# New planning figures and shorter turns in a planned convolution and gated feed-forward kernel

## The chip, the cores and the metric

The kernel runs on one core of a Trainium2 chip. The metric is the device time of one execution in microseconds (us). Before the change it is 1277.85 us, the median of three runs (1277.19, 1277.85 and 1282.22). Engines are named as in the profile: PE is TensorE (PEld its weight loads), DVE is VectorE, ACT is ScalarE, POOL is GpSimd, SP is SyncE, which here issues every DMA.

## The reference

Two stages follow each other. The first is a causal convolution whose seven weights are different at each position and head: a softmax over seven numbers, and with it a weighted sum of the last seven rows of `x`. The second is a gated feed-forward layer over the result.

```python
# x: (4, 4096, 192), weight_gen: (4, 4096, 8 heads, 7)
w = exp(weight_gen - max over the 7); w = w / (sum of w + 1e-9)
out[b, s, h] = sum over k of w[b, s, h, k] * x_pad[b, s + k, h]       # 24 channels a head
# x becomes (16384, 192); w_gate and w_val are (192, 1536), w_out is (1536, 192)
result = (sigmoid(x @ w_gate) * (x @ w_val)) @ w_out
```

## The kernel before

**Tiling.** The 16384 positions are cut into 32 blocks of 512. The 1536 hidden columns are cut into 12 groups of 128. A *unit* is one block with one group. The first groups of blocks 0 and 1 are done in halves of 256 positions, three groups of block 0 and four of block 1, so there are 391 units in all. Every fp32 operand of a matmul is split into a rounded value and its remainder, and a product takes three matmuls: a unit has 28 matmuls of 64 rows, which run as 14 pairs, one in the lower and one in the upper half of the array's rows.

**Stages of a block.** The convolution makes the block's inputs. DVE multiplies shifted slices of `x` by the weights (`prod`, L772; for the first positions L798) and adds the products (L710). For three early tiles the adding is done on PE, by matmuls with an identity matrix (`f_sum`, L720). The sums are then cast and split: channels 0 to 127 go to `A`, with the halves swapped to `As`, and the other 64 channels go to `T`. ACT casts (L828, L848, L875, L895), DVE subtracts to get the remainder (L831, L878), and ACT copies the remainder to the other rows (L851, L898). From block 4 on DMAs do the swaps.

**A period of PE.** PE takes one unit after another. In period s it makes gate and value of unit s (18 matmuls on `A`, `As`, `T`) and, beside them, the output products of unit s-3 (10 matmuls on `hh`, `hl`). Gate and value of a unit have a PSUM bank each (tiles `gv`), and there are two such pairs. So unit s can start only when ACT has read the gate of unit s-2 (sigmoid, L1041) and DVE has read its value (the product with the sigmoid, L1044). The product is cast to `hh` (ACT, L1047), and the remainder `hl` is a subtraction (DVE, L1050).

**Weights.** They arrive as 64-bit floats. Each of the 12 groups has a raw tile (`raw`, L410) that is turned into fp32 by 11 instructions: two on ACT (L419, L422), six on DVE (L426 to L457), one cast on ACT (L463) and two subtractions on DVE (L467), which leave the tile `W`.

**The softmax** of a stretch of positions is made on DVE and ACT (L516 to L555, exponential in L533) and stored to DRAM (`ws`, L584). The weights of a block come back spread over the heads' channels as `wb` and `wt` (L668).

**Turns.** Since the weights come one group at a time, the first two blocks take turns: block 0 does groups 0 to 6, then block 1 does groups 0 to 6, then block 0 the groups 7 to 11 and block 1 the same. From block 2 on a block does its 12 groups in one go. `TURN = 7` says so.

**What sets the order.** A planner (`Plan`) is run when the program is built. Every operation has a guessed duration on its engine, what it depends on, the buffers that it takes and a due time; the planner plays the program through with these guesses, and takes for each engine the operation that can start first, among those within 0.1 us of it the one due first. What comes out is a fixed order of instructions on each engine: an engine that meets an instruction whose input is missing waits, and all behind it wait with it. For DMAs the planner counts a start-up time, a bandwidth and an end time, and issues a load no more than `AHEAD` before the queue is expected to be free of the one before. The figures steer the order alone; no instruction takes another time because of them.

**Fills.** While a gap is planned on PE in the first 130 us, it is filled for 0.65 of its planned length by matmuls on a constant tile (`blank`): L628 before the first output products, L980 after.

Of the kernel before, what the change touches and what calls it, by code (L numbers as in the profile page):

```python
# [39 lines left out]
class Plan:  # L40
# [8 lines left out]
    SAME = {"pe": 0.0, "act": 0.05, "dve": 0.13, "pool": 0.1, "sp": 0.0}  # L49
    WINDOW = 0.1  # L50
    BANDWIDTH = 190e3
    DMA_START, DMA_END = 0.6, 1.0
    MARGIN, EARLY, LATE = 2.5, 60.0, 6.0
    AHEAD = 1.5
    TABLE = 1.28
    APART = 3

# [177 lines left out]
def conv_gated_ffn(ctx: ExitStack, tc: tile.TileContext, xt, wg, wcat, outT):  # L235
# [13 lines left out]
    P = 128  # L249
# [56 lines left out]
    def act(n, psum=False):  # L306
        return (0.05 if psum else 0.093) + 0.000835 * n
# [16 lines left out]
    def slot(n):  # L324
        return (n + 32) / 2400

    SP = 0.55
    RAW, WB = 0.6, 3.5

    def op(engs, fn, deps=(), **kw):  # L330

# [9 lines left out]
    EARLY_BLOCKS = 4  # L341
    FILL, WARM = 130.0, 4.8
    units = []
    TURN = 7
    spans = [(n, f, g) for f, g in ((0, TURN), (TURN, NF)) for n in range(2)]
    for n, first, end in spans + [(n, 0, NF) for n in range(2, NB)]:
        apart, cuts_ = parts(n)
# [272 lines left out]

    blank = sb.tile([P, 2 * N], F32R, name="blank")
    zero, ones = blank[:, :P], blank[:, N:]
    spare = plan.places["pt"][1]["buf"][:, M2:]
    begun = []

    def idle(buf, t):
        for _ in range(0 if begun else int(t / slot(K * CH))):
            nc.tensor.matmul(  # L628
                spare[:, : K * CH], ones[:, :P], ones[:, : K * CH], start=True, stop=True
            )  # L630

    def spread(key, chunks, sel, deps):
# [48 lines left out]
    def taps(key, groups, cols, mult, deps, uses, first=True, port=True, at=0, bank_of=None):  # L681
# [32 lines left out]
        if bank_of:  # L714
            for i, (k, z) in enumerate(groups):
                multiply(i)

                def f_sum(buf, e, i=i, k=k, z=z):
                    for j in range(k, z):
                        nc.tensor.matmul(  # L720
                            out(buf), eye[:, 0].bitcast(F32), flat(buf, i, j - k, j - k + 1),
                            start=j == 0, stop=j == K - 1,
                        )

                last = op(
                    {"pe": 0.1 + 0.00085 * (z - k) * cols}, f_sum, [ms[-1]] + ([last] if i else []),
                    alloc=[] if i else [(bank_of, ACC)], uses=[keys_[i]] + ([ACC] if i else []),
                )
                last.fill = idle
            return ACC, last  # L730
# [76 lines left out]
    def attention(n, a, z):  # L807
# [22 lines left out]
        def f_lo(buf, e):  # L830
# [3 lines left out]
            )  # L834

        hi = op(
            {"act": act(C)}, f_hi, last, alloc=[("A", A), ("As", As)] if new else [],
            uses=[ACC] + ([] if new else [A]),
        )
        lo = op(both(C), f_lo, [hi], uses=[A, ACC])  # L840
# [1 line left out]
        for rows, to in ((LOW, UP), (UP, LOW)):  # L842
            if n >= EARLY_BLOCKS:
                done.append(swap(A, As, all_, all_, rows, to, [lo]))
                continue

            def f_shi(buf, e, rows=rows, to=to):
                nc.scalar.copy(buf[As][to, 0, all_], buf[ACC][rows, :C])  # L848

            def f_slo(buf, e, rows=rows, to=to):  # L850
                nc.scalar.copy(buf[As][to, 1, all_], buf[A][rows, 1, all_].bitcast(F32))  # L851

            done.append(op({"act": act(C)}, f_shi, last, uses=[As, ACC], after=[hi]))
            done.append(op({"act": act(C)}, f_slo, [lo], uses=[A, As]))

        ready[q, 0], ready[q, 1] = [hi, lo], done

# [13 lines left out]
        for i, rows in enumerate((LOW, UP)):  # L871
            own = slice(a + i * M2, a + (i + 1) * M2)

            def f_thi(buf, e, rows=rows, own=own):
                nc.scalar.copy(buf[T][rows, 0, own], buf[ACT_][rows, :M2])  # L875

            def f_tlo(buf, e, rows=rows, own=own):
                ENG[e].tensor_tensor(  # L878
                    out=buf[T][rows, 1, own], in0=buf[ACT_][rows, :M2],
                    in1=buf[T][rows, 0, own].bitcast(F32), op=ALU.subtract,  # L880
                )

            fresh = new and not i
            his.append(
                op({"act": act(M2)}, f_thi, lastt, alloc=[("T", T)] if fresh else [],
                   uses=[ACT_] + ([] if fresh else [T]), after=his[-1:])
            )
            los.append(op(both(M2), f_tlo, [his[-1]], uses=[T, ACT_]))
            to = UP if i == 0 else LOW
            if n >= EARLY_BLOCKS:  # L890
                done.append(swap(T, T, own, own, rows, to, [los[-1]]))
                continue

            def f_shi(buf, e, rows=rows, to=to, own=own):
                nc.scalar.copy(buf[T][to, 0, own], buf[ACT_][rows, :M2])  # L895

            def f_slo(buf, e, rows=rows, to=to, own=own):
                nc.scalar.copy(buf[T][to, 1, own], buf[T][rows, 1, own].bitcast(F32))  # L898

            done.append(op({"act": act(M2)}, f_shi, lastt, uses=[T, ACT_], after=[his[-1]]))  # L900
            done.append(op({"act": act(M2)}, f_slo, [los[-1]], uses=[T]))
        ready[q, 2] = done + his + los


# [186 lines left out]
    def evac(n, done):  # L1091
# [19 lines left out]
            nc.sync.dma_start(out=outT[P:D, b * S + t0 : b * S + t0 + N], in_=buf[OT][LOW, :N])  # L1111

        t = due_block(n)
        h = op({"act": act(N, True)}, f_head, done, alloc=[("osb", OH)], uses=[PH], due=t + 8, lag=8)
        c = op({"act": act(N, True)}, f_shift, done, alloc=[("ev", EV)], uses=[PT], due=t + 10, lag=10)
        a = op({"dve": dve(N)}, f_fold, [c], port=False, alloc=[("osb", OT)], uses=[PT, EV], due=t + 14, lag=4)
        op({"sp": SP}, f_sth, [h], uses=[OH], nbytes=P * N * 4, due=t + 18, lag=10)
        op({"sp": SP}, f_stt, [a], uses=[OT], nbytes=R * N * 4, due=t + 20, lag=10)
# [89 lines left out]
```

## Time and profile before

| | |
|---|---|
| median of three runs | 1277.85 us |
| the profiled execution | 1276.69 us |
| its span, first to last instruction | 1274.9 us |
| PE busy | 1262.1 us, 99% of the span |
| DVE busy | 1010.1 us, 79% |
| ACT busy | 610.2 us, 48% |
| granted clock of PE | 0.999 of full speed |

The span is the stretch that the trace covers; the execution's own time is 1.8 us longer. DVE's 79% is a mean over two very different parts: it is busy for nine tenths or more of nearly every slice up to 300 us, and for seven to eight tenths behind that. POOL's 1499 instructions are almost all one-element writes that mark the change between the two halves of PE's rows (L958).

### The profile page before, as it was taken

The page shows a single profiled execution, that of the slowest core. Times are in us where ns is not written, and L with a number is a line of the kernel's source. Part 1 is how long each engine was busy: PE and PEld are TensorE (multiplying, and loading weights), DVE is VectorE, ACT ScalarE, POOL GpSimd, SP SyncE. Part 2 cuts the span into 40 slices and gives each one's busy share as a digit, 9 for nine tenths or more (in the row PEclk, how much of TensorE's full clock was granted, in tenths as well). Part 3 has the DMA queues.
Part 4 walks back from the last instruction along what each step waited for, and adds up shares of the span by engine and source line. Part 5 has one row for each costly group of instructions (what it writes and reads, how often), then busy time and mean ns, then how long its engine had stood idle before and what let it go on. Part 6 is the DMA issues. An engine that isn't in the chain of part 4 may idle for free.

```text
span 1274.9 us, 29675 instructions
## 1 busy us (share of the span) xinstructions
PE 1262.1 (99%) x11169; PEld 1124.4 (88%) x11169; DVE 1010.1 (79%) x1547; ACT 610.2 (48%) x1063; POOL 135.1 (11%) x1499
## 2 busy tenths in 40 slices
PE   8999999999999999999999999999999999999998
PEld 8887878888889999999999999999999999999997
DVE  8999999989998987788777788777778877755443
ACT  5766654454454644444444444444444444444443
POOL 0111111111111111111111111111111111111110
PEclk9999999999999999999999999999999999999999
DMA  8654687589878754454454454454454351011100
GB/s 237 198 117 110 149 168 144 154 171 180 169 143 207 156 148 111 113 137 105 104 123 107 113 137 111 99 123 108 111 137 117 92 129 35 20 32 38 38 14 13
DMA packets 44384, 150.37 MB, mean 118 GB/s; under 512 B 6288, under 2 KB 18896, under 8 KB 40400
## 3 DMA queue, kind: packets, MB, share of 16 engines
q1 hardware_dynamic: 44240, 148.48, 50.4%
q8 instruction: 87, 1.43, 0.5%
q14 instruction: 57, 0.47, 0.1%
HBM read 110.24 MB, written 16.20 MB: 99 GB/s over the span
## 4 chain that ended last, share of the span: by engine, by line
PE 87%; DVE 7%; ACT 2%; issue 1%; DMA 1%; SPq 0%; ACTq 0%; DVEq 0%; POOL 0%; POOLq 0%
PE bank L962 87%; DVE sg L1044 1%; DVE hl L1050 1%; DVE prod L772 1%; DVE prod L710 1%; DMA raw<-in_w 1%; DVE W L467 0%; DVE ce L451 0%; DVE ce L457 0%; ACT As L851 0%; DVE ch L439 0%; ACT hh L1047 0%; PE bank L720 0%; DMA w<-in_weight_gen 0%; ACT sg L1041 0%
## 5 line engine op out<-in xcount | busy, mean ns | idle before, releaser
L962 PE MATMUL bank<-hh,W 64*128 64x512 f32 (+1 forms) x2346 | 771.1, 383 | 0.3 <-POOL seen L958 0.3
L962 PE MATMUL bank<-T,W 64*128 64x512 f32 (+1 forms) x2346 | 646.6, 382 | 0.4 <-ACT T L898 0.4
L962 PE MATMUL bank<-As,W 64*128 64x512 f32 (+1 forms) x2346 | 646.9, 383 | 0.0
L962 PE MATMUL bank<-hl,W 64*128 64x512 f32 (+1 forms) x1564 | 595.6, 382 | 0.1
L1047 ACT CAST hh<-sg 128x512 fp32r<-128x512 f32 (+1 forms) x391 | 239.8, 614 | 545.4 <-DVE sg L1044 544.9
L962 PE MATMUL bank<-A,W 64*128 64x512 f32 (+1 forms) x2346 | 476.9, 384 | 2.3 <-ACT sg L1041 1.2
L962 PEld LDWEIGHTS bank<-hh,W 64*128 64x128 f32 x2346 | 429.2, 184 | 29.3 <-POOL seen L958 1.6
L962 PEld LDWEIGHTS bank<-T,W 64*128 64x128 f32 x2346 | 427.1, 184 | 28.0 <-ACT T L898 0.6
L962 PEld LDWEIGHTS bank<-As,W 64*128 64x128 f32 x2346 | 427.1, 184 | 27.1
L1044 DVE TENSOR_TENSOR sg<-bank,sg 128x512 f32<-128x512 f32 (+1 forms) x391 | 264.1, 676 | 154.7 <-PE bank L962 152.1
L1050 DVE TENSOR_TENSOR hl<-sg,hh 128x512 fp32r<-128x512 f32 (+1 forms) x391 | 263.9, 675 | 92.4 <-ACT hh L1047 90.3
L962 PEld LDWEIGHTS bank<-A,W 64*128 64x128 f32 x2346 | 299.4, 184 | 33.6 <-DVE sg L1044 2.7
L962 PEld LDWEIGHTS bank<-hl,W 64*128 64x128 f32 x1564 | 287.4, 184 | 18.8 <-DVE hl L1050 0.6
L1041 ACT ACTIVATE sg<-bank 128x512 f32<-128x512 f32 (+1 forms) x391 | 230.4, 590 | 82.2 <-PE bank L962 76.1
L958 POOL MEMSET seen<- 1x1 f32 x1493 | 134.3, 90 | 1133.2 <-PE bank L962 1130.7
L772 DVE TENSOR_TENSOR prod<-x,wb 128x1024 f32<-128x1024 f32 x126 | 135.5, 1076 | 0.5 <-DMA wb<-ws 0.5
L710 DVE TENSOR_TENSOR prod<-prod,prod 128x1024 f32<-128x1024 f32 (+2 forms) x94 | 103.7, 1103 | 0.0
L772 DVE TENSOR_TENSOR prod<-xt,wt 128x1024 f32<-128x1024 f32 (+1 forms) x66 | 68.4, 1041 | 1.8 <-DMA wt<-ws 1.7
L710 DVE TENSOR_TENSOR acc<-prod 128x512 f32<-128x512 f32 (+2 forms) x64 | 32.6, 539 | 0.7
L878 DVE TENSOR_TENSOR T<-acc,T 64x256 fp32r<-64x256 f32 (+1 forms) x66 | 26.7, 404 | 1.2 <-ACT T L875 0.2
L875 ACT CAST T<-acc 64x256 fp32r<-64x256 f32 (+1 forms) x66 | 26.0, 394 | 1.0
L1103 DVE TENSOR_TENSOR osb<-bank,ev 64x512 f32<-64x512 f32 x32 | 21.5, 673 | 4.4 <-ACT ev L1100 4.4
(62 smaller groups left out, 381.8 us busy)
## 6 DMA issues: line engine op xcount, KB each, us to landing
wb<-ws SPq DMA_DIRECT2D x30, 1792.0 KB
wt<-ws SPq DMA_DIRECT2D x60, 448.0 KB
As<-A SPq DMA_DIRECT2D x56, 256.0 KB
out<-osb SPq DMA_DIRECT2D x32, 256.0 KB
x<-in_x SPq DMA_DIRECT2D x30, 259.0 KB
T<-T SPq DMA_DIRECT2D x56, 128.0 KB
raw<-in_w SPq DMA_DIRECT2D x12, 575.8 KB
out<-osb SPq DMA_DIRECT2D x32, 128.0 KB
```

The source lines that it names most:

```text
L710: nc.vector.tensor_tensor(out=dst(buf), in0=a(buf), in1=b(buf), op=ALU.add)
L772: nc.vector.tensor_tensor(out=dst.rearrange("p (k j t) -> p k j t", k=z - k, t=L), in0=sliding(buf[X][:, k : k + cols], z - k, [[L, cols / ...
L875: nc.scalar.copy(buf[T][rows, 0, own], buf[ACT_][rows, :M2])
L878: ENG[e].tensor_tensor(out=buf[T][rows, 1, own], in0=buf[ACT_][rows, :M2], in1=buf[T][rows, 0, own].bitcast(F32), op=ALU.subtract,)
L958: turn = nc.gpsimd.memset(seen, 0.0)
L962: ins = nc.tensor.matmul(buf[dst][:, c:d], w, m[:, c:d], start=start, stop=stop)
L1041: nc.scalar.activation(out=buf[k["sg"]][:, a:z], in_=buf[k["g"]][:, a:z], func=AF.Sigmoid)
L1044: nc.vector.tensor_tensor(out=buf[k["sg"]][:, a:z], in0=buf[k["v"]][:, a:z], in1=buf[k["sg"]][:, a:z], op=ALU.mult)
L1047: nc.scalar.copy(buf[k["hh"]][:, a:z], buf[k["sg"]][:, a:z])
L1050: ENG[e].tensor_tensor(out=buf[k["hl"]][:, a:z], in0=buf[k["sg"]][:, a:z], in1=buf[k["hh"]][:, a:z].bitcast(F32), op=ALU.subtract)
L1103: nc.vector.tensor_tensor(out=buf[OT][LOW, :N], in0=buf[PT][LOW, :N], in1=buf[EV][LOW, :N], op=ALU.add)
```

## The change

Most of it sets figures of the planner. Sums on PE are planned at `0.25 + 0.0017` us a column where it was `0.1 + 0.00085`. Casts of ACT in the convolution get 0.08 us more, the two copies of a finished output block 0.12 us more. A DMA's planned start-up goes from 0.6 to 1.3 us and its end from 1.0 to 1.2 us. `AHEAD` goes from 1.5 to 3.0. `TURN` goes from 7 to 6, so blocks 0 and 1 do groups 0 to 5 first and 6 to 11 later. The tile that the fills write (`spare`) is now looked up among four banks, leaving out one that holds an open sum.

```diff
-    DMA_START, DMA_END = 0.6, 1.0
+    DMA_START, DMA_END = 1.3, 1.2
-    AHEAD = 1.5
+    AHEAD = 3.0
-    RAW, WB = 0.6, 3.5
+    RAW, WB, MORE = 0.6, 3.5, 0.08
-    TURN = 7
+    TURN = 6
-    spare = plan.places["pt"][1]["buf"][:, M2:]
-    begun = []
+    spares = [b["buf"] for t in ("pt", "ph") for b in plan.places[t]]
+    begun, opened = [], []
     def idle(buf, t):
-        for _ in range(0 if begun else int(t / slot(K * CH))):
+        spare = [b for b in spares if not any(b is o for o in opened)]
+        for _ in range(0 if begun or not spare else int(t / slot(K * CH))):
...
                 def f_sum(buf, e, i=i, k=k, z=z):
+                    if i == 0:
+                        opened.append(buf[ACC])
+                    else:
+                        opened[:] = [o for o in opened if o is not buf[ACC]]
...
-                    {"pe": 0.1 + 0.00085 * (z - k) * cols}, f_sum, [ms[-1]] + ([last] if i else []),
+                    {"pe": 0.25 + 0.0017 * (z - k) * cols}, f_sum, [ms[-1]] + ([last] if i else []),
...
-            {"act": act(C)}, f_hi, last, alloc=[("A", A), ("As", As)] if new else [],
+            {"act": act(C) + MORE}, f_hi, last, alloc=[("A", A), ("As", As)] if new else [],
...
-        h = op({"act": act(N, True)}, f_head, done, alloc=[("osb", OH)], uses=[PH], due=t + 8, lag=8)
+        h = op({"act": act(N, True) + 0.12}, f_head, done, alloc=[("osb", OH)], uses=[PH], due=t + 8, lag=8)
```

What the program does is the same on every engine: the same matmuls, casts, subtractions and DMAs, apart from the fills (L628: 115 before, 95 now; L980: 38 before, 24 now). Their order is another. Three places matter below. Lines behind L620 have moved by 1 to 5.

First DVE, around the first remainder of `T` (tile `T_85`, L878, now L883), at the start of block 0. `x_64`, `wb_71`, `xt_66` and `wt_73` belong to the second half of block 0; `W_308` and `W_251` are the weights of group 0. Before:

```order
L772 TENSOR_TENSOR prod_76<-x_64,wb_71 128x1024
L831 TENSOR_TENSOR A_81<-bank,A_81 128x256
L467 TENSOR_TENSOR W_308<-ce_102,W_308 128x512
L467 TENSOR_TENSOR W_308<-ce_102,W_308 128x64
L772 TENSOR_TENSOR prod_77<-x_64,wb_71 128x768
L772 TENSOR_TENSOR prod_75<-xt_66,wt_73 128x512
L772 TENSOR_TENSOR prod_76<-xt_66,wt_73 128x384
L878 TENSOR_TENSOR T_85<-bank,T_85 64x128 x2
```

and now:

```order
L836 TENSOR_TENSOR A_81<-bank,A_81 128x256
L551 RECIPROCAL m_69<-m_69 128x32
L467 TENSOR_TENSOR W_251<-ce_102,W_251 128x512
L555 TENSOR_TENSOR w_67<-w_67,m_69 128x224
L467 TENSOR_TENSOR W_251<-ce_102,W_251 128x64
L883 TENSOR_TENSOR T_85<-bank,T_85 64x128 x2
L457 TENSOR_TENSOR ce_104<-ce_104,ch_108 128x576
L467 TENSOR_TENSOR W_314<-ce_103,W_314 128x512
L467 TENSOR_TENSOR W_314<-ce_103,W_314 128x64
L426 TENSOR_SCALAR cu_111<-cu_111 128x576
L467 TENSOR_TENSOR W_357<-ce_104,W_357 128x512
L777 TENSOR_TENSOR prod_76<-x_64,wb_71 128x1024
```

The four products of the second half stood ahead of the first `T`; now they stand behind it, and behind the weights of groups 1 and 2.

Second ACT, where block 2 begins, the first block behind the turns. `sg_88`, `sg_89` and `sg_87` are here the units 28, 29 and 30, the last three of block 1; `A_81`, `As_83` and `T_85` are the inputs of block 2. Before:

```order
L828 CAST A_81<-acc_79 128x512
L848 CAST As_83<-acc_79 64x512 x2
L1041 ACTIVATE sg_89<-bank 128x512
L1047 CAST hh_90<-sg_88 128x512
L875 CAST T_85<-acc_80 64x256 x2
L851 CAST As_83<-A_81 64x512 x2
L895 CAST T_85<-acc_80 64x256
L898 CAST T_85<-T_85 64x256
...
L1047 CAST hh_91<-sg_89 128x512
L1041 ACTIVATE sg_87<-bank 128x512
```

and now:

```order
L833 CAST A_81<-acc_79 128x512
L853 CAST As_83<-acc_79 64x512 x2
L880 CAST T_85<-acc_80 64x256 x2
L1052 CAST hh_90<-sg_88 128x512
L856 CAST As_83<-A_81 64x512 x2
L900 CAST T_85<-acc_80 64x256
L903 CAST T_85<-T_85 64x256
...
L1046 ACTIVATE sg_89<-bank 128x512
L1046 ACTIVATE sg_87<-bank 128x512
L533 ACT_TABLE_LOAD
L533 ACTIVATE w_67<-w_67 128x896
```

The sigmoid of unit 29 (`sg_89`) has moved from behind the third cast to behind the last, and the switch to the exponential (the table load, L533) follows two rows later.

Third SP, in the first microseconds. `raw_...` are the weights of a group, `ws_119` is the softmax of the second half of block 0, which `wb_71` and `wt_73` bring back. Before:

```order
L410 DMA raw_154<-in_w 128x2303
L410 DMA raw_158<-in_w 128x2303
L380 DMA x_64<-in_x 128x262
L380 DMA xt_66<-in_x 64x134
L505 DMA w_67<-in_weight_gen 128x224
L584 DMA ws_119<-w_68 128x112
L380 DMA xt_66<-in_x 64x134
L410 DMA raw_242<-in_w 128x2303
L668 DMA wb_71<-ws_119 128x1x1792
L584 DMA ws_120<-w_67 128x224
L668 DMA wt_73<-ws_119 64x1x896 x2
```

and now:

```order
L410 DMA raw_152<-in_w 128x2303
L410 DMA raw_155<-in_w 128x2303
L380 DMA x_64<-in_x 128x262
L380 DMA xt_66<-in_x 64x134 x2
L410 DMA raw_171<-in_w 128x2303
L410 DMA raw_179<-in_w 128x2303
L584 DMA ws_119<-w_68 128x112
L505 DMA w_67<-in_weight_gen 128x224
L410 DMA raw_248<-in_w 128x2303
L410 DMA raw_272<-in_w 128x2303
L669 DMA wb_71<-ws_119 128x1x1792
L669 DMA wt_73<-ws_119 64x1x896 x2
```

One raw tile stood between `x_64` and `wb_71`, now there are four, two of them ahead of the softmax's store `ws_119`. In the same way more loads go ahead of their use at later places.

## Rows read from the trace of the kernel before

**Rows 1.** The page, part 1: busy us (share) and count of each engine.

```profile
PE 1262.1 (99%) x11169; PEld 1124.4 (88%) x11169; DVE 1010.1 (79%) x1547; ACT 610.2 (48%) x1063; POOL 135.1 (11%) x1499
```

**Rows 2.** Windows: stretch, length, busy us (records) of PE, PEld, DVE, ACT, POOL; clock, DMA.

```profile
20.00:120.00 100.00, 96.26 (x944) 82.61 (x944) 95.04 (x199) 67.85 (x144) 10.88 (x110) 1.00 0.66 167
160.00:180.00 20.00, 19.38 (x166) 15.46 (x164) 19.74 (x28) 10.31 (x17) 1.92 (x21) 1.00 0.77 159
200.00:1200.00 1000.00, 1000.00 (x8826) 898.74 (x8824) 790.79 (x1146) 458.23 (x781) 107.54 (x1206) 1.00 0.51 117
1270.00:1275.00 5.00, 0.00 (x0) 0.00 (x0) 0.68 (x1) 0.92 (x2) 0.00 (x0) 0.70 0.25 79
```

**Rows 3.** Timeline of PE: start, length, line, operation, [idle before <-releaser].

```profile
16.90 1.47 PE L720 MATMUL bank<-prod,eye 128*128 128x256 f32 x6
...
23.66 0.62 PE L962 MATMUL bank<-A,W 64*128 64x256 f32 x6
...
27.63 0.39 PE L962 MATMUL bank<-T,W 64*128 64x256 f32 x2 [0.40 <-ACT T L898]
...
33.99 0.78 PE L962 MATMUL bank<-A,W 64*128 64x256 f32 x5 [0.55 <-ACT sg L1041]
```

**Rows 4.** Timeline of DVE, block 0.

```profile
20.47 1.22 DVE L772 TENSOR_TENSOR prod<-x,wb 128x1024 f32<-128x1024 f32 x1
...
22.67 0.95 DVE L772 TENSOR_TENSOR prod<-x,wb 128x768 f32<-128x768 f32 x1
25.31 1.16 DVE L772 TENSOR_TENSOR prod<-xt,wt 128x512 f32<-128x512 f32 x2 [1.69 <-DMA wt<-ws]
26.39 0.60 DVE L878 TENSOR_TENSOR T<-bank,T 64x128 fp32r<-64x128 f32 x2
```

**Rows 5.** Timeline of DVE, block 2 begins.

```profile
118.01 0.86 DVE L878 TENSOR_TENSOR T<-acc,T 64x256 fp32r<-64x256 f32 x2
118.91 0.69 DVE L1044 TENSOR_TENSOR sg<-bank,sg 128x512 f32<-128x512 f32 x1
...
120.11 0.95 DVE L516 TENSOR_REDUCE m<-w 128x64 f32<-128x448 f32 x1
...
122.58 1.15 DVE L523 TENSOR_TENSOR w<-w,m 128x448 f32<-128x448 f32 x2
```

**Rows 6.** Timeline of ACT, block 2 begins.

```profile
113.93 0.62 ACT L828 CAST A<-acc 128x512 fp32r<-128x512 f32 x1 [0.35 <-DVE acc L710]
...
115.85 0.60 ACT L1041 ACTIVATE sg<-bank 128x512 f32<-128x512 f32 x1
...
120.29 0.40 ACT L898 CAST T<-T 64x256 fp32r<-64x256 f32 x1
```

**Rows 7.** Timeline of PE, the first period of block 2.

```profile
119.62 0.86 PE L980 MATMUL bank<-blank 64*128 64x512 f32 x4
120.09 0.86 PE L962 MATMUL bank<-A,W 64*128 64x512 f32 x5
```

**Rows 8.** Timeline of ACT, where block 3 begins.

```profile
156.80 0.59 ACT L1041 ACTIVATE sg<-bank 128x512 f32<-128x512 f32 x1
157.41 1.28 ACT L533 ACT_TABLE_LOAD   x1
158.70 0.95 ACT L533 ACTIVATE w<-w 128x896 f32<-128x896 f32 x1
...
161.48 1.08 ACT L1041 ACTIVATE sg<-bank 128x512 f32<-128x512 f32 x2
```

**Rows 9.** Timeline of PE, where block 3 begins.

```profile
162.13 0.50 PE L962 MATMUL bank<-A,W 64*128 64x512 f32 x1 [0.39 <-ACT sg L1041]
162.86 0.74 PE L962 MATMUL bank<-A,W 64*128 64x512 f32 x4 [0.23 <-DVE sg L1044]
```

**Rows 10.** Timeline of SP: the first load of spread weights.

```profile
11.69 0.58 SPq L668 DMA_DIRECT2D wb<-ws  x1
```

**Rows 11.** The chain that ended last, 0 to 40 us: start, length, what.

```profile
18.38 7.39 DMA raw<-in_w
```

More of the change, by code (lines that the diff above doesn't have):

```diff
@@ L622, in conv_gated_ffn @@
     zero, ones = blank[:, :P], blank[:, N:]
-    spare = plan.places["pt"][1]["buf"][:, M2:]
-    begun = []
+    spares = [b["buf"] for t in ("pt", "ph") for b in plan.places[t]]
+    begun, opened = [], []
     def idle(buf, t):
-        for _ in range(0 if begun else int(t / slot(K * CH))):
+        spare = [b for b in spares if not any(b is o for o in opened)]
+        for _ in range(0 if begun or not spare else int(t / slot(K * CH))):
             nc.tensor.matmul(
-                spare[:, : K * CH], ones[:, :P], ones[:, : K * CH], start=True, stop=True
+                spare[-1][:, CT // 2 : CT // 2 + K * CH], ones[:, :P], ones[:, : K * CH], start=True, stop=True
             )
@@ L851, in f_slo @@
                 nc.scalar.copy(buf[As][to, 1, all_], buf[A][rows, 1, all_].bitcast(F32))
-            done.append(op({"act": act(C)}, f_shi, last, uses=[As, ACC], after=[hi]))
-            done.append(op({"act": act(C)}, f_slo, [lo], uses=[A, As]))
+            done.append(op({"act": act(C) + MORE}, f_shi, last, uses=[As, ACC], after=[hi]))
+            done.append(op({"act": act(C) + MORE}, f_slo, [lo], uses=[A, As]))
         ready[q, 0], ready[q, 1] = [hi, lo], done
@@ L884, in attention @@
             his.append(
-                op({"act": act(M2)}, f_thi, lastt, alloc=[("T", T)] if fresh else [],
+                op({"act": act(M2) + MORE}, f_thi, lastt, alloc=[("T", T)] if fresh else [],
                    uses=[ACT_] + ([] if fresh else [T]), after=his[-1:])
@@ L898, in f_slo @@
                 nc.scalar.copy(buf[T][to, 1, own], buf[T][rows, 1, own].bitcast(F32))
-            done.append(op({"act": act(M2)}, f_shi, lastt, uses=[T, ACT_], after=[his[-1]]))
-            done.append(op({"act": act(M2)}, f_slo, [los[-1]], uses=[T]))
+            done.append(op({"act": act(M2) + MORE}, f_shi, lastt, uses=[T, ACT_], after=[his[-1]]))
+            done.append(op({"act": act(M2) + MORE}, f_slo, [los[-1]], uses=[T]))
         ready[q, 2] = done + his + los
@@ L1113, in evac @@
         t = due_block(n)
-        h = op({"act": act(N, True)}, f_head, done, alloc=[("osb", OH)], uses=[PH], due=t + 8, lag=8)
-        c = op({"act": act(N, True)}, f_shift, done, alloc=[("ev", EV)], uses=[PT], due=t + 10, lag=10)
+        h = op({"act": act(N, True) + 0.12}, f_head, done, alloc=[("osb", OH)], uses=[PH], due=t + 8, lag=8)
+        c = op({"act": act(N, True) + 0.12}, f_shift, done, alloc=[("ev", EV)], uses=[PT], due=t + 10, lag=10)
         a = op({"dve": dve(N)}, f_fold, [c], port=False, alloc=[("osb", OT)], uses=[PT, EV], due=t + 14, lag=4)
```

## The prediction

> **What bounds the kernel now.** First the page's shares: PE is busy 99% of the span, DVE 79%, ACT 48% [rows 1]. So time is won only where PE stands still, works on fills, or works slower than it can. Second the windows, to see where that is. From 200 to 1200 us PE runs 8826 records in 1000 us without a gap [rows 2]; a period of 28 matmuls thus takes 28 / 8.826 = 3.17 us. Third a count: 32 blocks by 12 groups, the halves counted as halves, are 384 periods, 384 x 3.17 = 1218 us. The first matmul on A starts at 23.66 us [rows 3] and nothing runs on PE from 1270 [rows 2], 1246 us later. Some 28 us are therefore neither useful matmuls nor start and tail. They hold sums on PE, pairs of unlike length in the halves, fills and waits, and all of them lie ahead of 180 us, since behind that every period takes its 3.17. The change can win from these 28 us and from the first 23.66, and no more.
>
> What sets PE's pace there is DVE: from 20 to 120 us it is busy 95.04 of 100 us [rows 2]. Its idle 4.96 us are waits, the largest one of 1.69 us for `wt` [rows 4]. I read the new order against that: if DVE does the same work with fewer waits, all that hangs on it comes earlier.
>
> **The first T.** Before, DVE ends the first remainder of T at 26.39 + 0.60 = 26.99 us [rows 4], and PE's matmuls on T follow at 27.63 [rows 3]. Up to that instruction the new order holds the same DVE instructions but four: the products of the second half, which now come later. From start to start of what follows they take 1.13 (20.47 on), about 0.87 (22.67 on: 0.95 less the 0.08 by which neighbours overlap) and 1.08 us (25.31 to 26.39, two of them), and the 1.69 us of waiting for `wt` lie among them [rows 4]. 26.99 - 3.08 - 1.69 = 22.2 us, so PE comes to T at about 23.2 and group 1 follows without the gap. This is not a gain yet. The four products have to be done for the second half, whose first period starts at 33.99 behind a wait of 0.55 [rows 3]; up to its T the new DVE order even holds six more instructions, four of a conversion and two of a unit, for which I estimate about 2 us from their sizes, so that this T is ready when it was. What stays is that 2 us of DVE's waiting have become work.
>
> **Block 2.** Up to the last remainder of T of block 2, 118.01 + 0.86 = 118.87 us [rows 5], both DVE orders hold the same instructions, but for one `hl` that now comes behind (0.60). If DVE waited nowhere, it would be there 4.96 + 0.60 = 5.6 us earlier; if it waits as much as now, 0.6 earlier. Between these ends I take waits of 0.8 us: the 1.69 go, as the products no longer stand ahead of a T while `wt` is on its way, and what I find left by following the order are short waits for values that PE has not finished. That makes 118.87 - 0.60 - 4.16 = 114.1 us.
>
> PE does not get all of it. Before, ACT takes the sigmoid of unit 29 at 115.85, in the middle of the casts of block 2 that run from 113.93 to 120.69 [rows 6]; DVE's product follows right behind T at 118.91, and PE starts block 2 at 120.09, behind four fills [rows 5, 7], 1.2 us after the T. In the new order the sigmoid stands behind the last cast, and DVE's product of it behind `hl` (0.60), the fold of an output block (from the end of 118.91's product to 120.11, 0.60), a reduction (0.87) and two subtractions (together 1.06, 122.58 to 123.64) [rows 5]. The product thus ends 3.13 + 0.60 = 3.7 us after T. PE needs it, because the value bank of unit 29 is the one that block 2's first period takes. ACT comes out the same: the casts (6.2 us without the sigmoid between them) begin 3.6 us ahead of T's end, six DVE instructions being between, and with the sigmoid's 0.6 they end 3.2 us after it. With six fills, three pairs of 0.23, that wait for the same bank, PE starts block 2 about 4.6 us after T: at 118.7 instead of 120.09. **Gain 1.4 us**; 3.4 of DVE's 4.8 us are given back at this one place.
>
> **Block 3.** Before, ACT takes the sigmoid of unit 41 only at 156.80, behind the last casts of block 3, and then changes tables for the exponential at 157.41 and back; the next sigmoids start at 161.48 [rows 8], and PE waits for them at 162.13 and 162.86 [rows 9]. From 160 to 180 us it has 166 records where 20 x 8.826 = 176.5 would fit: 10.5 / 8.826 = 1.2 us lost [rows 2]. In the new order the same instructions stand there in the same sequence, but DVE comes to block 3 some 3 us earlier against PE's periods than it did, so the casts of block 3 are over when unit 41's gate is done. The sigmoid and both table changes then move ahead by over 2 us against PE, and the wait of 1.2 us has room to vanish. Its bounds are 0 and 1.2; I take 1.2, as the lead is twice the wait. **Gain 1.2 us.**
>
> The row puts ACT's next work 0.01 us behind the load's 1.28 (157.41 to 158.70) [rows 8]. [...]
>
> **What costs or gives nothing.** The planner's figures change no instruction. The 20 plus 14 matmuls of fills that go lie in waits that PE has anyway, so their price is 0; were they in PE's way, 34 of them would give back at most some 2 us. Sums on PE have the same matmuls and keep their time. Loads issued further ahead are hidden behind DVE's queue of work as long as they come in time; the second rival is where they don't. Between 60 and 80 us both orders hold a table switch amid the second block's halves, and I find PE's waits there alike (about 3 us). Turns of six let block 1 begin one period earlier and put six conversions in place of five into the stretch behind it; that is in DVE's count above. Behind 180 us nothing waits now, and the tail is the same instructions.
>
> **Sum.** 1.4 + 1.2 = 2.6 us. The profiled execution took 1276.69 us, which makes 1274.1. It is 1.16 under the median of the three runs, so for that median I forecast 1275.2 us.
>
> **Rivals.**
> *The waits vanish altogether.* If ACT takes the sigmoids in time at block 2 and at the switch between 60 and 80 us, DVE's whole lead reaches PE: 4.8 + 1.2 + about 3 = 9 us, 1268.9 us. For it: DVE's lead is there to be had. Against it: the new ACT order, in which the sigmoid of unit 29 stands behind all casts. Chance 0.14.
>
> *The weights' loads come in the way.* Four raw tiles now stand ahead of `wb_71`, two of them ahead of the softmax's store; before it was one. `wb` was issued at 11.69 [rows 10] and DVE used it at 20.47 without a wait [rows 4]. Where three raw tiles and two `wt` were on the way together, one raw took 7.39 us [rows 11]. If each of the three additional tiles holds up `wb_71` and the two `wt` behind it by a third of that, 2.5 us, these come 7.4 us later than before, `wt` at about 32.7, where the new order wants it at about 26.5. DVE stands for 6 us instead of 1.7, and the 4.96 us that were to be won become a loss of some 4; block 3's wait stays as well. That is 1277.85 + 4 to 5 = 1282 us. It decides as soon as `wt` lands later than about 27 us. Against it: at that time SP had free stretches before, and the tiles are issued 4 us earlier than `raw_242` was. Chance 0.13.
>
> *PE's clock falls at the start.* PE idles more between 8 and 22 us, because 18 fills between the two spreads are gone. [...] Chance 0.06.
>
> *The change moves the waits and no more:* what block 2 and 3 win is lost between 80 and 110 us, where six conversions instead of five now compete with the units' two DVE instructions a period. 1277.5 us. Chance 0.07.
>
> **How the numbers follow.** The forecast has 0.60; its own range is 1272 to 1278.5, from DVE's waits taken as 0 to 3 us. The 80% range takes in half of either outer case: 1269 to 1282. Runs of this kernel differ by some 0.4%, so a difference under 0.5%, 6.4 us, can't be told from none: faster means under 1271.5, slower over 1284.2. Faster: most of the first rival and an edge of the forecast, 0.14. Slower: the upper third of the second rival, 0.06. Within: 0.80.
>
> **What would show it.** Right: DVE idle under 2 us from 20 to 120 us; first matmul on T near 23; block 2's first matmul on A near 118.7, the sigmoid before it behind the last cast of T; no wait at 160. Wrong: a wait of DVE for `wb` or `wt` of over 1 us near 25, a granted clock under 1 before 25, new waits of PE behind 180 us, or block 2 starting within 2 us of its T.

## The result

The changed kernel takes 1289.12 us (median of 4 runs, 1288.05 to 1289.94), the kernel before, run beside it, 1278.48 us (4 runs). The ratio is 1.0082, with a 95% interval of 1.0066 to 1.0099: slower by 10.6 us between the medians, where the forecast was 1275.2 and the range ended at 1282. The profiled execution took 1289.94 us, 13.25 more than the profiled one of before; that is 2.6 more than the medians differ by, as the first is the slowest of its four runs and the second, at 1276.69, is below the fastest of its own.

I read the profile after in the order in which the one of before was read. First the shares:

```profile
PE 1262.7 (98%) x11135; PEld 1214.6 (94%) x11135; DVE 1010.6 (78%) x1547; ACT 611.9 (47%) x1063; POOL 133.5 (10%) x1499
```

PE, DVE, ACT and POOL have the same busy time as before to within 2 us [rows 1]. Only PE's weight loads (PEld), which run beside its matmuls, are busy for 90 us more; why stays open, and it costs nothing, as PE's pace below shows. So no work was added on an engine; 13 us in which PE stands or runs slowly were. The windows say where (columns as in [rows 2]):

```profile
20.00:120.00 100.00, 95.15 (x921) 80.56 (x919) 96.21 (x203) 67.32 (x142) 10.68 (x110) 1.00 0.67 155
160.00:180.00 20.00, 20.00 (x180) 16.37 (x178) 19.85 (x26) 10.38 (x18) 2.04 (x23) 1.00 0.80 149
198.00:204.00 6.00, 1.18 (x11) 0.64 (x7) 4.77 (x7) 1.02 (x2) 0.15 (x2) 1.00 0.85 172
204.00:209.00 5.00, 0.00 (x0) 0.00 (x0) 0.00 (x0) 0.00 (x0) 0.00 (x0) 0.50 0.98 150
209.00:214.00 5.00, 4.87 (x24) 3.68 (x26) 0.00 (x0) 1.10 (x2) 0.26 (x3) 0.50 0.81 154
220.00:1220.00 1000.00, 1000.00 (x8825) 985.93 (x8824) 785.65 (x1138) 459.15 (x778) 106.45 (x1207) 1.00 0.48 114
```

From 160 to 180 us PE now has 180 records instead of 166 [rows 2]: the wait at block 3 is gone. From 220 us the pace is that of before, 8825 records in 1000 us against 8826 [rows 2]. Between them stands something new: from 199 to 209 us PE does nothing, from 204 on at a granted clock of 0.50, and after it has begun again the clock stays at 0.50 until 214. The list of waits from 195 to 215 us (engine, line, what it waited for: us in all, times, longest) names the reason:

```profile
PE bank L967 <- DMA As<-A: 10.0, 1, 10.0
```

The chain that ended last, followed back from 215 us (start, length, what), goes through the same transfer:

```profile
172.03 14.26 DMA x<-in_x
...
186.30 22.78 DMA As<-A
...
209.13 6.07 PE bank L967 x28
```

`As` of block 4 is the first one that comes by DMA and not by ScalarE's casts (`EARLY_BLOCKS = 4`). It takes two swaps, and the second one was issued at 186.30 and was there 22.78 us later. What stood ahead of it is seen in SyncE's timeline. First the kernel before, whose rows of this place were not needed until now:

```profile
173.88 0.54 SPq L668 DMA_DIRECT2D wb<-ws  x1
184.46 1.15 SPq L787 DMA_DIRECT2D As<-A  x2
185.71 2.08 SPq L787 DMA_DIRECT2D T<-T  x2
...
188.50 0.62 SPq L668 DMA_DIRECT2D wt<-ws  x1
...
195.33 0.62 SPq L668 DMA_DIRECT2D wt<-ws  x1
```

Then SyncE in the changed kernel:

```profile
173.18 0.59 SPq L669 DMA_DIRECT2D wb<-ws  x1
...
179.30 0.61 SPq L669 DMA_DIRECT2D wt<-ws  x1
...
183.92 0.61 SPq L669 DMA_DIRECT2D wt<-ws  x1
185.34 1.44 SPq L792 DMA_DIRECT2D As<-A  x2
186.89 9.56 SPq L792 DMA_DIRECT2D T<-T  x2
```

Before, the two `wt` loads of block 6 were issued behind the swaps of block 4; now they are issued ahead of them. The swaps of `As` are issued within a microsecond of the old time. PE wants `As` 13 us after that; the first product that DVE makes with the two `wt` loads starts at 228.45, 44 us after the second load's issue.

The 13.25 us add up. They are read from the starts of block 4's first periods in PE's timeline. First before:

```profile
197.72 0.84 PE L962 MATMUL bank<-A,W 64*128 64x512 f32 x5
```

Then in the changed kernel, the starts of the first, second and third period:

```profile
198.12 0.84 PE L967 MATMUL bank<-A,W 64*128 64x512 f32 x5
...
213.99 0.98 PE L967 MATMUL bank<-A,W 64*128 64x512 f32 x5
...
217.31 0.64 PE L967 MATMUL bank<-A,W 64*128 64x512 f32 x4
```

The first period of block 4 starts at 198.12 instead of 197.72: 0.40 us from everything ahead of it. That period takes 15.87 us and the next 3.32, together 19.19 or 12.85 more than two of 3.17. Of these 10.1 are the gap (from the start of one matmul to that of the next 10.3 us, less the 0.23 of an ordinary step), and 2.7 are matmuls at half the clock.

### The profile page after: what moved, and what is told of

It is laid out like the page before. It is cut to its first block, busy times and chain, and to the rows that moved or that the text cites. A ratio compares the mean times of both kernels' runs of the same rounds, so it can differ in the third digit from the quotient of the medians.

```text
span 1288.2 us, 29587 instructions
## 1 busy us (share of the span) xinstructions
PE 1262.7 (98%) x11135; PEld 1214.6 (94%) x11135; DVE 1010.6 (78%) x1547; ACT 611.9 (47%) x1063; POOL 133.5 (10%) x1499
## 4 chain that ended last, share of the span: by engine, by line
PE 85%; DVE 7%; DMA 5%; ACT 2%; issue 1%; SPq 0%; ACTq 0%; DVEq 0%; POOL 0%; POOLq 0%
PE bank L967 85%; DMA As<-A 2%; DVE prod L777 1%; DMA xt<-in_x 1%; DMA x<-in_x 1%; DVE sg L1049 1%; DVE hl L1055 1%; DVE prod L711 0%; DVE W L467 0%; DVE ce L457 0%; DMA w<-in_weight_gen 0%; ACT sg L1046 0%; DVE ch L439 0%; ACT As L853 0%; DVE m L516 0%
## 5 line engine op out<-in xcount | busy, mean ns | idle before, releaser
L967 PE MATMUL bank<-As,W 64*128 64x512 f32 (+1 forms) x2346 | 648.3, 383 | 10.2 <-DMA As<-A 10.0
L967 PEld LDWEIGHTS bank<-A,W 64*128 64x128 f32 x2346 | 312.7, 184 | 13.3 <-DVE sg L1049 1.6
L883 DVE TENSOR_TENSOR T<-acc,T 64x256 fp32r<-64x256 f32 (+1 forms) x66 | 26.7, 404 | 2.9 <-ACT T L880 1.9
```

The costliest lines, as they stand in the source:

```text
L883: ENG[e].tensor_tensor(out=buf[T][rows, 1, own], in0=buf[ACT_][rows, :M2], in1=buf[T][rows, 0, own].bitcast(F32), op=ALU.subtract,)
L967: ins = nc.tensor.matmul(buf[dst][:, c:d], w, m[:, c:d], start=start, stop=stop)
```

## The experiments

My theory after reading the traces: the swaps of block 4 stand behind the `wt` loads in SyncE's DMA queue, which alone makes the wait; the lower clock is its consequence; the rest of the change is about neutral. The rivals: the DMA engines are simply full from 173 to 209 us; the casts of block 4 come late; turns of six, or the prices of sums and casts, are what costs.

**The swaps first.** The changed kernel, with the order of the planner constrained at this one place; no other engine's order changes.

```
+        if n == 6:
+            for s in ready[(n - 2, 0), 1] + ready[(n - 2, 0), 2][:2]:
+                wt[0].after.append(s); s.succ.append(wt[0])
```

> The changed kernel with one edit: the two wt loads of block 6 are issued behind the four swaps of block 4, as before the change; the order on TensorE, VectorE and ScalarE is the same. Theory (the swaps of block 4 stand behind the two wt loads in SyncE's queue, and TensorE waits 10.3 us for As and then runs 10.2 us at the lower clock): As is there when TensorE comes to it at 198.8, no wait and no lower clock at 204, so the time falls by 10.3 + 2.4 = 12.7 us to about 1276.4. Rival A (the DMA engines are simply full from 173 to 209 us, whatever the order): half of the wait or more stays, 1283 or above. Rival B (the casts and remainders of block 4's A come late): nothing changes, 1289.

Measured: 1278.45 us (10 runs) against 1278.85 of before, ratio 0.9997 (0.9986 to 1.0009). PE takes block 4 at 198.79 without a wait, as its windows show:

```profile
198.00:204.00 6.00, 6.00 (x56) 5.37 (x54) 6.00 (x11) 2.71 (x5) 0.62 (x7) 1.00 1.10 197
204.00:214.00 10.00, 10.00 (x91) 9.43 (x90) 9.94 (x16) 5.42 (x11) 0.98 (x11) 1.00 1.01 138
```

The wait and the fall of the clock behind it are gone with three lines, which refutes both rivals: the same bytes are loaded, and A's casts are where they were. It came out 2 us above the 1276.4 expected, and this kernel's trace shows where such a difference lies. Block 4 starts 0.67 later in it, with the same order ahead: from 12 to 16 us the granted clock was 0.57 on average here and 1.00 in the changed kernel's trace. And PE waits 1.3 us for DVE's products at 336 and 366 us, which the changed kernel does not. (Of the 10.2 us at the lower clock that the expectation names, PE works in the last 5 only.)

**The loads first, in the kernel before.** The opposite edit there: the swaps of block 4 wait for the issue of `wt`.

```
+        if n == 6:
+            for s in ready[(4, 0), 1] + ready[(4, 0), 2][:2]:
+                s.after.append(wt[1]); wt[1].succ.append(s)
```

> The kernel before with one edit: the four swaps of block 4 are issued behind the two wt loads of block 6; no other engine's order changes, and none of the planner's figures. Theory: the wait of the changed kernel appears here too, near 198 us, some 8 to 13 us with the lower clock behind it, 1286 to 1291. Rivals (turns of six, or the figures of sums and casts, make the wait; or the DMA engines' load as a whole): within 2 us of the kernel before, 1277 to 1280.

Measured: 1291.35 us, ratio 1.0097 (1.0073 to 1.0120), 0.35 above the expected range. The wait and the lower clock are there, in a kernel with none of the change's figures. Its list of waits has:

```profile
PE bank L962 <- DMA As<-A: 11.3, 1, 11.3
```

Its window behind the fall of the clock:

```profile
204.00:214.00 10.00, 3.46 (x16) 2.49 (x18) 0.00 (x0) 0.29 (x1) 0.18 (x2) 0.50 1.02 170
```

So, with all of these DMAs in SyncE's queue, the order at this place is both needed and enough for the loss.

**Work through the wait.** 42 pairs of matmuls with zero weights ahead of the first matmul on `As` of block 4.

```
+                    if t == ("As", EARLY_BLOCKS) and dst[0] == "gv" and not stood:
+                        stood.append(1)
+                        for _ in range(42):
+                            for i, r in enumerate((LOW, UP)):
+                                nc.tensor.matmul(buf[dst[0], dst[1], i], zero[r], ones[r], start=False, stop=False)
```

> The changed kernel with 42 pairs of matmuls that add zeros (42 x 0.23 = 9.5 us) put ahead of the first matmul on As of block 4, so that TensorE works through the wait. Theory: As still lands at about 209.1 and the wait's remainder is under 1 us; the granted clock stays at 1.00 behind it, so 2.4 us come back: about 1286.7. Rival (the lower clock is not caused by the stop, or costs nothing): the clock still falls near 204 and the time stays at 1289.

Measured: 1288.53 us (4 runs, 1286.16 to 1290.81), ratio 1.0068 (1.0050 to 1.0086). The median is not far enough from 1289.12 to tell by itself. The trace tells: the clock stays up, and block 4's first two periods take 16.24 us (13.07 and 3.17) instead of 19.19, 2.95 less. Its windows:

```profile
198.00:204.00 6.00, 6.00 (x56) 4.98 (x54) 4.35 (x7) 0.62 (x1) 0.09 (x1) 1.00 0.86 154
204.00:214.00 10.00, 10.00 (x89) 8.06 (x89) 2.88 (x6) 3.03 (x6) 0.62 (x7) 1.00 0.88 167
```

Of these 2.95, 0.2 is that the two periods lose 9.9 us here and lost 10.1 to the gap there, and 2.7 is the clock, as much as the sum above has for it. So the stop caused the fall of the clock, and that is what filling it gives back.

**Another queue.** The `wt` loads stay ahead; block 4's swaps are issued by ScalarE.

```
-            nc.sync.dma_start(
+            (nc.scalar if key_in[1] == 4 else nc.sync).dma_start(
```

> The changed kernel with the four swaps of block 4 issued from ScalarE's DMA queue instead of SyncE's; the two wt loads stay where they are. Theory (a DMA queue is worked off in order, so the swaps wait for the loads ahead in the same queue): As lands well before 198 us, no wait, about 1276.4. Rival A (the DMA engines are full, the order in the queue doesn't matter): the swaps still land behind 203 us and at least 5 us of wait stay, 1283 or above.

Measured: 1284.15 us, ratio 1.0035 (1.0022 to 1.0049). The time lies in the rival's range, but not for the rival's reason. PE has no wait for `As` any more, and one of 1.39 us for `T`; so the packets of the swaps did pass the loads. But the time was lost anew, on ScalarE (start, length, line, operation, [idle before <-releaser]):

```profile
186.42 0.66 ACTq L792 DMA_DIRECT2D T<-T  x1
187.13 0.60 ACT L1046 ACTIVATE sg<-bank 128x512 f32<-128x512 f32 x1 [0.67 <-PE bank L967]
193.86 0.62 ACTq L792 DMA_DIRECT2D T<-T  x1
194.52 0.62 ACT L1052 CAST hh<-sg 128x512 fp32r<-128x512 f32 x1 [6.80 <-DMA wb<-ws]
```

The last swap of T is not issued before the load of `wb` has landed, and on ScalarE a cast and the next sigmoids stand behind it for 6.8 us; PE waits for them, and its granted clock is 0.50 from 198 to 201 us (matmuls 0.43 us apart instead of 0.23). In the changed kernel SyncE has the same wait (the second T there is issued at 195.85), but nobody's casts are behind it. My expectation named the packets rightly and forgot what is queued behind a waiting issue. That the DMA engines were not full is seen in the changed kernel itself, in its windows around the wait:

```profile
184.00:190.00 6.00, 6.00 (x56) 4.94 (x56) 5.96 (x10) 2.24 (x4) 0.62 (x7) 1.00 0.98 179
190.00:196.00 6.00, 6.00 (x56) 4.98 (x54) 6.00 (x9) 2.23 (x4) 0.71 (x8) 1.00 0.50 108
196.00:202.00 6.00, 3.18 (x29) 2.28 (x25) 6.00 (x10) 1.74 (x3) 0.35 (x4) 1.00 0.67 143
```

From 190 to 202 us the 16 DMA engines are busy for 0.50 and 0.67 of the time (the column before the last), while half of the packets of `As` are still standing in the queue. In the run with the swaps on ScalarE their 448 packets are listed under a queue of their own, and the last packet of `As` started at 195.0, while `wt` went on to 203.1. The second half of the packets of `As` moved only from 191.0 on, when the load of `wb` in SyncE's queue was all but done (its last packet started at 192.2).

**Where the other half of the engines was.** From 200 to 202 us only packets of `wt` moved, 33 of 486 ns on average: 33 x 0.486 / 2 = 8.0 engines of 16. `wt` is read as 8 copies of 8 rows, `wb` as 16 copies. This kernel reads the two loads of block 6 as plain rows instead, which leaves out that block's right weights; the order is untouched.

```
-            src = bass.AP(
+            src = bass.AP(w.tensor, w.offset, [[K * cols, reps * H], [1, K * cols]]) if key == ("wt", (6, 0)) else bass.AP(
```

> The changed kernel, its order untouched, with the two wt loads of block 6 read as 64 plain rows in place of 8 copies of 8 rows; block 6 so gets other weights than it should (that part of the result is left out), in the same bytes and packets. From 200 to 202 us only packets of wt moved, 33 of 486 ns each, which is 33 x 0.486 / 2 = 8.0 of the 16 engines. Theory (a load that begins with 8 copies sits on 8 engines, and half of As stands behind it there while the others are free): spread over all engines the 128 packets take 128 x 0.486 / 16 = 3.9 us instead of 7.8, As lands some 4 to 6 us earlier, the wait falls from 10.3 to 4 to 6 us and the clock falls later or not at all: 1279 to 1284. Rival (the share of 0.50 has another reason, such as the memory that is read): the wait stays at 9 us or more, 1288 or above.

Measured: 1287.53 us (1285.50 to 1290.76), ratio 1.0083 (1.0059 to 1.0108): by the time, no better than the changed kernel, and outside what I expected. In its trace the share of the engines is as the theory has it, and the wait is 4 us shorter, and no more. First its windows:

```profile
190.00:196.00 6.00, 6.00 (x56) 5.32 (x54) 6.00 (x9) 2.24 (x4) 0.67 (x8) 1.00 0.94 165
196.00:202.00 6.00, 2.54 (x23) 1.89 (x19) 6.00 (x11) 1.74 (x3) 0.30 (x4) 1.00 0.94 162
```

Then its list of waits:

```profile
PE bank L967 <- DMA As<-A: 6.3, 1, 6.3
```

Block 4's first two periods take 15.38 us here instead of 19.19, and the granted clock falls all the same (0.56 on average from 202 to 208 us). That the two `wt` loads, which begin with 8 copies, sat on half the engines is shown by the two shares from 190 to 196 us, 0.50 as copies and 0.94 as plain rows. By this trace it makes 4 of the 10.3 us. The other 6 stay, as there are still two halves: 64 of the 128 packets of `As` start by 195.5 us and the other 64 only from 198.5 on, behind `wb`, which has landed at 196.1, and half of the packets of `wt`. Why the median of the four timed runs, 1.6 us under the changed kernel's, doesn't show the 4 us stays open.

**The planner's figures one at a time.** Four kernels each undo or do one of them. What SyncE's order has ahead of block 4's swaps follows from the plan and was known before the run.

```
-    AHEAD = 3.0
+    AHEAD = 1.5
```

> The changed kernel with one of the planner's figures as before: loads go 1.5 us ahead instead of 3.0; sums, casts, landing times and turns of six stay. SyncE's order then has the swaps of block 4 ahead of both wt loads. Theory (only the order of these two against the swaps costs): no wait of TensorE on As, within 0.3% of the kernel before, 1276 to 1282. Rival (the other figures bring the wait or another as long): 1285 or more.

Measured: 1280.22 us, ratio 1.0003 (0.9991 to 1.0016), no wait on `As`.

```
-    TURN = 6
+    TURN = 7
```

> The changed kernel with turns of seven groups as before, all other figures as changed. SyncE's order then has one wt load of block 6 ahead of the swaps of block 4 and one behind. Theory (packets ahead in the same queue): half of the packets stand ahead, the wait for As is 2 to 5 us instead of 10.3, so short that the granted clock hardly falls: 1280 to 1284. Rival (any load ahead of the swaps costs the whole wait): 1288 or more; rival (a single load is hidden): 1277 to 1279.5.

Measured: 1281.53 us, ratio 1.0019 (1.0002 to 1.0035). The time is in the expected range and for another reason: there is no wait on `As` at all. `wt` is issued at 176.44 and `As` at 181.40 here, and block 4 begins at 200.23, so one load ahead is hidden, as the second rival had it. The 2 us are lost at block 2, whose start comes at 123.39 and whose first two periods are preceded by 5.3 us of waits and fills.

```
-    TURN = 7
+    TURN = 6
```

> The kernel before with turns of six groups and nothing else. SyncE's order keeps the swaps of block 4 ahead of the wt loads. Theory (turns of six are not what costs): no wait on As near 198, within 0.3% of the kernel before, 1275 to 1282. Rival (turns of six crowd the conversions, and that is the loss): 1285 or more.

Measured: 1278.93 us, ratio 0.9998 (0.9984 to 1.0013), no wait of PE's matmuls on `As` (its weight loads wait 0.4 us for it, so it came just in time). Turns of six, in the kernel before, cost and give nothing.

```
-                    {"pe": 0.25 + 0.0017 * (z - k) * cols}, f_sum, [ms[-1]] + ([last] if i else []),
+                    {"pe": 0.1 + 0.00085 * (z - k) * cols}, f_sum, [ms[-1]] + ([last] if i else []),
```

> The changed kernel with the planner's price of the sums on TensorE as before (0.1 + 0.00085 a column instead of 0.25 + 0.0017), all else as changed. SyncE's order keeps both wt loads of block 6 ahead of the swaps of block 4. Theory: the wait for As is there as in the changed kernel, 8 to 11 us with the lower clock behind it, 1286 to 1291. Rival (the longer price of the sums makes the loss): within 0.3% of the kernel before.

Measured: 1290.46 us, ratio 1.0090 (1.0068 to 1.0112), with a wait of 7.4 us on `As`; its block 2 starts 2.3 us later than the changed kernel's, so the wait finds PE later.

```
-    DMA_START, DMA_END = 1.3, 1.2
+    DMA_START, DMA_END = 0.6, 1.0
```

> The changed kernel with the planner's landing times of a load as before (0.6 and 1.0 us instead of 1.3 and 1.2), loads still going 3.0 us ahead. SyncE's order keeps both wt loads of block 6 ahead of the swaps of block 4. Theory: the wait for As stays, 1286 to 1291. Rival (the longer landing times make it): within 0.3% of the kernel before, 1275 to 1282.

Measured: 1290.53 us, ratio 1.0088 (1.0063 to 1.0113), with a wait of 11.3 us on `As`.

So two of the changed figures have to be there together for the loss: `AHEAD = 3.0`, which lets loads go further ahead, and turns of six. With either one as before the wait is gone. The prices of sums and the landing times are not needed; the 0.08 us for casts and the 0.12 for copies were not tried alone. In all orders tried, PE stands over 6 us for `As` exactly where both loads go ahead in the same queue, but for the run that fills this time with useless matmuls.

**Block 2's sigmoid.** The forecast had put block 2's start down to the sigmoid of unit 29, behind all casts. This kernel takes it ahead of the last six, and keeps the swaps of blocks 4 and 5 first.

```
+        if n in (6, 7):
+            for s in ready[(n - 2, 0), 1] + ready[(n - 2, 0), 2][:2]:
+                wt[0].after.append(s); s.succ.append(wt[0])
...
+        if s == 29:
+            for x in ready[(2, 0), 1][1::2] + ready[(2, 0), 2][:4]:
+                x.after.append(o); o.succ.append(x)
```

> The changed kernel with the wt loads of blocks 6 and 7 behind the swaps of blocks 4 and 5, and with the casts of block 2's second copies planned behind the sigmoid of unit 29, so that ScalarE takes this sigmoid ahead of the last six casts instead of behind them. Theory (block 2's start is set by that sigmoid and VectorE's product of it, not by T): the sigmoid moves from 120.15 to about 117.6, the product to about 118.9, and TensorE starts block 2 near 119.9 instead of 121.84, so 2 us less than the kernel with the loads moved alone: about 1276.5, TensorE without a wait at 198. Rival (VectorE's queue or block 3 takes it back): block 2 starts earlier, but the time stays at 1278.5.

Measured: 1276.48 us (12 runs) against 1278.40, ratio 0.9978 (0.9965 to 0.9992). It is faster than both kernels, by little. The planner's other choices move with the edit, so the orders of DVE and ACT differ at other places too; that the 2 us come from this one is read at the start of block 2, 1.87 us earlier. ScalarE's timeline in the changed kernel, the sigmoids behind the casts:

```profile
120.15 1.07 ACT L1046 ACTIVATE sg<-bank 128x512 f32<-128x512 f32 x2
```

And in this one, the sigmoid of unit 29 first:

```profile
117.48 0.59 ACT L1046 ACTIVATE sg<-bank 128x512 f32<-128x512 f32 x1
...
120.41 0.40 ACT L903 CAST T<-T 64x256 fp32r<-64x256 f32 x1
```

PE's timeline where block 2 begins, in the changed kernel:

```profile
120.79 1.44 PE L985 MATMUL bank<-blank 64*128 64x512 f32 x6 [0.94 <-ACT sg L1046]
121.84 0.62 PE L967 MATMUL bank<-A,W 64*128 64x512 f32 x3
```

And in this one:

```profile
119.52 0.84 PE L985 MATMUL bank<-blank 64*128 64x512 f32 x4
119.97 0.39 PE L967 MATMUL bank<-A,W 64*128 64x512 f32 x1
```

## Why the prediction was wrong, point by point

**The step that failed** is a sentence under "What costs or gives nothing": "Behind 180 us nothing waits now, and the tail is the same instructions", with an earlier one there, that loads issued further ahead are hidden as long as they come in time. This put the new order of loads behind 180 us at nothing; it cost 12.85 us. The loads that went ahead at block 4 did come in time. I asked of each load who waits for it, and not what is issued behind it in the same queue. "New waits of PE behind 180 us" stands among the prediction's own signs of being wrong, but no price was put on them. The second rival, on the weights' loads, had the right mechanism, loads that come in the way of what stands behind them, but at the start, for `wb` and `wt`, where no wait came of it: DVE has none on a DMA from 20 to 120 us now. The order of SyncE at block 4 could be read beforehand, and `As` is named there as the first tile that comes by DMA. The prediction looks at SyncE's order only at the start. Nothing else in the sum was of this size: 10.1 us of standing and 2.7 of the lower clock. The rest came to a loss of 0.4 us where a gain of 2.6 was forecast.

**The first T** was right to within a microsecond, and PE's part of it closer by luck. DVE ends its remainder at 22.81 + 0.29 = 23.10 us, 0.9 later than the forecast 22.2, and PE begins on T 0.35 later, at 23.45, where a step of 1.0 was taken to 23.2. PE's timeline has it:

```profile
21.10 0.38 PE L967 MATMUL bank<-A,W 64*128 64x256 f32 x2
...
23.45 0.71 PE L967 MATMUL bank<-T,W 64*128 64x256 f32 x6
...
34.07 0.50 PE L967 MATMUL bank<-A,W 64*128 64x256 f32 x4
```

That this is not yet a gain was right too: the second half's first period starts at 34.07, before at 33.99 [rows 3].

**Block 2** was mis-sized, in one term. DVE's waits from 20 to 120 us were taken to fall from 4.96 to 0.8 us; they are 100 - 96.21 = 3.79. That is 3.0 of the 3.5 us by which T's last remainder ends later than forecast, at 116.75 + 0.88 = 117.63 instead of 114.1:

```profile
116.75 0.88 DVE L883 TENSOR_TENSOR T<-acc,T 64x256 fp32r<-64x256 f32 x2
```

The wait for `wt` is gone as expected, and one as long has come in its place. At 50 us ScalarE waits for the raw tile of a conversion, with the casts of T in its queue behind it:

```profile
50.10 0.72 ACT L419 COPY ch<-raw 128x576 bf16<-128x576 bf16 x1 [2.50 <-DMA raw<-in_w]
50.73 0.62 ACT L880 CAST T<-acc 64x128 fp32r<-64x128 f32 x2
```

DVE in turn waits for these casts, with the remainders of T:

```profile
51.05 0.61 DVE L883 TENSOR_TENSOR T<-acc,T 64x128 fp32r<-64x128 f32 x2 [1.94 <-ACT T L880]
```

No run takes this wait away alone; that it cost block 2 its lead is read from the trace only. The other half of the step held: PE starts block 2 at 121.84, 4.2 us after T's end, where 4.6 were forecast, and the run with the sigmoid first showed that it is the sigmoid that sets it, within 0.1 us of its expectation for PE (119.97 against 119.9). With T only 1.2 us earlier than before and 4.2 instead of 1.2 us behind it, block 2 starts 1.75 us later than before, not 1.4 earlier.

**Block 3** was right in the number, and in part by luck: the wait is gone. From the first matmul of its first period to that of its third, PE took 165.98 - 158.19 = 7.79 us before and takes 166.38 - 159.94 = 6.44 now, 1.35 won where 1.2 were forecast. But DVE's lead at this place did not come from DVE being early: PE had started block 2 late. Nor did unit 41's sigmoid move ahead by over 2 us against PE: it starts at 157.26 where it was 156.80 [rows 8], which against PE's delay of 1.75 is 1.3 us, just enough. -1.75 and +1.35 make the 0.40 us by which block 4 starts later.

**The other rivals.** In the changed kernel's trace the granted clock was 1.00 from the start to 204 us, so the clock at the start has no part in its 13.25 us. The rival is not out for good: in the trace of the run with the swaps first, whose start has the same order, the clock was 0.57 from 12 to 16 us and block 4 came 0.67 later. That the waits only move was nearest for the first 198 us: net 0.4 us. That they vanish was wrong for the change, and the run with the sigmoid first got 2 us of those 9.

## What to carry to other kernels

A load that is early enough for its own reader can still be too early, as the two `wt` here, which cost 12.85 us: ask of every DMA what is issued behind it in the same queue and how soon that is needed, at each place where the order of the two turns round. In SyncE's queue here, the swaps that the bounding engine wanted 13 us later should have gone ahead of loads that were first used 44 us later. The same question holds for an engine's own queue: a conversion that waited 2.50 us for its raw tile held up the casts behind it, as a swap on ScalarE did for 6.8 us.

## What the runs showed of the hardware

While half of the packets of `As` stood in SyncE's queue behind the loads, the DMA share was 0.50 (190 to 196 us), and the same swaps from ScalarE's queue passed the `wt` loads (last packet of `As` at 195.0, of `wt` at 203.1). In the changed kernel half of the packets of `As` (64 of 128, each of 4096 bytes) moved from 186.6 to 190.0 us, ahead of the two `wt` that were issued before them. The other half moved only from 202.7 to 207.5, when all but 3 of the 128 packets of 7168 bytes of the two `wt` (193.9 to 203.5) had started. The landings say the same: the trace marks each of the two swaps of `As` as landed in 16 steps, 8 of them by 191.2 us and 8 from 205.9 on. So half of `As` passed the loads ahead of it in the queue and half waited for them, where my theory had the whole queue in order. That the half which waited shares engines with the loads is my reading of the shares; which of the 16 engines took which packets the records don't say. The kernel before was close to this already: there, too, half of the packets of `As` came late (193.3 to 196.0 us, behind `wb`), and PE began on `As` at 198.40. The two `wt`, which begin with 8 copies, kept 8 engines busy from 200 to 202 us (33 x 0.486 / 2 = 8.0); read as plain rows, they went at a share of 0.94 (196 to 202 us).

A stop of PE of 10.3 us cost 2.7 us more than its length: the granted clock fell to 0.50 while PE stood and was still 0.50 for the first 5 us in which it worked again. With 42 pairs of useless matmuls in the gap it stayed at 1.00.

The last of four DMA issues in a row waited until an earlier, unrelated load had landed: 8.3 us on SyncE in the changed kernel, 6.8 us on ScalarE in the run with its queue. The traces show why, and it is a wait that the program sets: its 410 DMAs signal their landing on eight semaphores that they take in turn, and an issue waits until the DMA that had its semaphore before, the eighth ahead of it, has landed. For the second swap of T that one is the load of `wb`, in both runs. On ScalarE a cast and the next sigmoids stood behind it for those 6.8 us.
